# Finishing pieces, transfers, half down tiles and banks: a finer order around an attention loop

## The chip, the cores and the metric

The kernel runs on one core of a Trainium2 chip. The time is device time of one execution, in microseconds (us); for the kernel before it is the median of three runs. One execution was also recorded by the hardware profiler. The engines are named as the profile names them: PE (TensorE, matrix products), PEld (its weight loads), DVE (VectorE), ACT (ScalarE), POOL (GpSimd) and SP (SyncE, which here only issues transfers; "SPq" is its queue). L384 is line 384 of the kernel.

## The reference

The inputs are bf16: x of 2048 rows by 448, caches of 8 key and value heads (2048 keys by 256), and weights. Attention uses 16 query heads, two to each key head, and only the last 512 keys.

```
xn = layernorm(x)
q  = (xn @ wq) as 16 heads of 256
p  = softmax(q @ k.T / 16)                 # k: the last 512 keys
s  = concat_over_heads(p @ v) @ wo
g  = silu((gelu(xn @ w_gate) * (xn @ w_up)) @ w_down)
out = x + s * g
```

## The kernel before

Three stages follow one another. Everything is written into one list of operations by `K.op`, which works out the waits; each engine then runs its own operations in the order of the list. So the order in the code is the order on each engine, and an operation that waits holds up all that stands behind it on its engine, SP's queue included.

**Stage 1, up to about 119 us**: layernorm, the gate and up products and their gelu, with the transposed xn stored to DRAM.

**Stage 2, about 119 to 159 us**, is set by the tuple `order` (L981) and the loop over it (L989). For each head h, `vw_head` computes V_h @ Wo_h (512 x 448), so that the attention later multiplies its probabilities with this and gets the output of wo at once. A head is eight matmuls of 128x448 in four PSUM banks. `vw_mm` (L707) copies them out: of banks j = 0 and j = 1, ACT copies one half and DVE the other less the first (L713, L715); banks j = 2 and 3 are copied by ACT (L719). The banks are filled in the order j = 0, 2, 1, 3. `vw_sums` (L723) then makes three further blocks on DVE. Between the heads stand the last down products of the feed-forward part: tile t of 128 rows is 14 matmuls (`down_mm`, L569), then a tanh on ACT and one DVE operation that make its gate (`down_gate`, L574); `store_g` (L564) sends the gate to DRAM. In `order` a pair is two heads, a float half a down tile, a negative number a whole tile. Heads 14 and 15 come last, with the queries of the first two steps between them.

**Stage 3, about 159 to 551 us**, is the loop of NST = 128 steps (L1037): 8 chunks c of 256 rows (two tiles), 16 heads h each, n = 16 c + h. PE is used as two halves of 64 rows that run side by side; `halves` (L796) deals the matmuls of a step to both. In step n stand on PE the scores of n (`s_jobs`, banks 4 to 6 in turn), the queries of n + 2 (`q_jobs`) and the products of probabilities and V Wo of step m = n - 4 (`pv_jobs`). The 2 x 2 blocks of a product are formed with seven products instead of eight; they need four sums or differences of the probabilities (`sums`, L878, DVE) and are added up over the 16 heads of a chunk in banks 0 to 3: p = 1, 2 in bank 0, p = 6, 7 in bank 1, p = 4, 5 in bank 2, p = 3 in bank 3. In a chunk's first step they start with bank 0, then bank 2 in one half.

The other engines, per step: DVE takes two row minima (L852), the reciprocal of step n - 1's sums (L863) and the sums of step n - 3; ACT takes the copy of the queries and two exponentials (L857); POOL normalises the probabilities of step n - 1 in two instructions (L873); SP issues their transpose (`dma_t`, L375), which step n + 3 uses in its products.

A chunk *ends* at step 16 c + 19, when its last head's products are done. The banks are copied (`evac`, L939, in that step), and `finish` (L947) lists nine pieces, run in the steps after: four POOL additions, a DVE piece `fin(1)` (L962, product with the gate), a POOL piece `add(1)` (L972, plus x), a POOL addition, `fin(0)`, `add(0)`. A step takes a DVE piece from the front of the list, if one is there, behind its sums, and at its end a POOL piece, if one is there. So a DVE piece and the POOL piece behind it fall in one step, and the nine pieces take seven steps. POOL pieces wait for the step's last sum (`after=last_sum`). `add` marks a tile ready; two steps later `store_out` (L934) issues the store of the tile and, through `load_fin` (L930), the two loads (x rows and gate) of the tile four on. At step 4 (`n == LAG`) `load_fin` is called for tiles 0 to 3: eight loads at once. Behind step 115's chunk four steps (118 to 121) also have one more addition each on DVE (`vw_plain`, L1023).

In steps 0 to 3 there are no products yet. There the last two tiles' down products (tiles 14 and 15, half a tile per step) take their place, in bank 0 and 1, and the second half of the queries of steps 2 to 5 goes to bank 3 (the first half to bank 7).

The last chunk's last four products (steps 124 to 127) are done plainly in the tail (L1148), both tiles for each step, in banks 7 and 5; then a product and an addition per tile, DVE and POOL for tile 0, DVE and DVE for tile 1, and the two stores. Of step 127 the two tiles are transposed apart.

Of the kernel before, what the change touches and what calls it, by code (L numbers as in the profile page):

```python
# [166 lines left out]
def bass_recurrent_scan__sliding_block_cached__geglu_ffn__prompt_kernel(  # L167
# [12 lines left out]
    _, S, D = A_x.shape  # L180
# [5 lines left out]
    NT = S // P  # L186
    QC = 512
    NQC = S // QC
    NF = F // P
# [14 lines left out]
    with es:  # L204
# [166 lines left out]
        def dma(q, o, i, reads=(), writes=()):  # L371
            K.op(q, lambda e, o=o, i=i: e.dma_start(o, i), reads, writes, dma=True)  # L372
# [437 lines left out]
        def q_jobs(n, e):  # L810

            c, h = divmod(n, Hq)
            y, i = c % 2, bq(n)
            if e == 1 and 2 <= n < 2 + LAG:
                i = 3
            out = ([], [])
            reads = b_wql[h // HG] + [b_xq[y]]
            for u in range(2):
                rows = slice(R * u, R * u + R)
                for k in [2, 1, 0] + ([NK] if u == e else []):  # L820
                    l = wqr[rows, h, :] if k == NK else wq[rows, k, h * Dh + e * P:h * Dh + (e + 1) * P]
                    out[u].append([i, e * CW, (e + 1) * CW, l, xq[rows, y, k, :], False, False, reads])
            return out

        def q_evac(n):
            s, i = n % NQT, bq(n)
            if 2 <= n < 2 + LAG:
                for e, i in ((0, 7), (1, 3)):
                    act(qT[:, s, e, :], bank[i][:, e * CW:(e + 1) * CW], ACT.Copy, (b_ps[i],), b_qT[s][e:e + 1], scale=NEG)
            else:  # L830
                act(qT[:, s, :, :].rearrange("p e q -> p (e q)"), bank[i], ACT.Copy, (b_ps[i],), b_qT[s], scale=NEG)
# [95 lines left out]
        def load_xq(c):  # L927
            dma("sp", xq[:, c % 2, :, :], xnd[c, :, :, :], b_xnd[2 * c:2 * c + 2], (b_xq[c % 2],))

        def load_fin(t):  # L930
            dma("sp", xr[:, t % NXR, :], x_view[:, t, :], (), (b_xr[t % NXR],))
            dma("sp", gr[:, t % NXR, :], gd[t, :, :], (b_gd[t],), (b_gr[t % NXR],))

        def store_out(t):  # L934
            dma("sp", out_view[:, t, :], ofin[:, t % 2, :], (b_ofin[t % 2],), ())
            if t + NXR < NT:
                load_fin(t + NXR)

# [39 lines left out]
                    ("dve", fin(0)), (eng, add(0))]  # L978


        order = (8.0, (3, 4), 8.5, (5, 6), -9, (7, 8), -10, (9, 10), -11, (11, 12), -12, (2, 13), -13, 14, 15)  # L981
        ring = [0]

        def banks4():
# [2 lines left out]
            return r  # L987

        for k in order:  # L989
            if isinstance(k, tuple):  # L990
                vw_head(k[0], banks4())
                vw_head(k[1], banks4())
                if k[0] in (7, 9):
                    y = k[0] // 8
                    K.reuse(b_xq[y:y + 1])
                    load_xq(y)
            elif isinstance(k, float):
                f = 0 if k == 8 else NF // 2
                down_mm(8, bank[4][:, 0:D], [b_ps[4]], f, f + NF // 2)
                if f:  # L1000
                    down_gate(8, bank[4][:, 0:D], [b_ps[4]])
                    store_g()
            elif k < 0:
                i = 4 + k % 2
                down_tile(-k, bank[i][:, 0:D], [b_ps[i]])
                store_g()
# [30 lines left out]
        for n in range(NST):  # L1037
# [8 lines left out]
            for t in ready:  # L1046
                store_out(t)
            ready, stores = stores, []
            if more:
                q0, q1 = q_jobs(n + 2, 0), q_jobs(n + 2, 1)  # L1050
                q0[1][0][5] = True
                (q1[0] if m >= 0 else q1[1])[-1][6] = True
                if m < 0:
                    q1[0][0][5] = q0[0][-1][6] = True
            if m < 0:
                halves(s0[0] + q1[0] + q0[0] + s1[0], q0[1] + s1[1] + s0[1] + q1[1])
                t, i, f = NT - 2 + n // 2, n // 2, n % 2 * NF // 2
# [44 lines left out]
        assert not todo and not stores and not ready  # L1102

        def add(eng, o, a, b, reads, writes, f=ALU.add):
            K.op(eng, lambda e: e.tensor_tensor(o, a, b, f), reads, writes)
# [39 lines left out]
        add("dve", o, o, gs[1], b_aS[4:6] + b_tmp[1:2], b_aS[4:6], ALU.mult)  # L1145
        add("dve", o, o, xs[1], b_aS[4:6] + [b_xr[ends_at[1]]], b_aS[4:6])
        PB = (7, 5)
        for n in range(NST - LAG, NST):  # L1148
            h, x = n % Hq, n % NPT
            v = vw[:, vslot(h), :, :, :]  # L1150
            for t in range(2):
                i = PB[t]
                mms([(bank[i][:, 0:D].rearrange("p (a n) -> p a n", a=2), pT[:, x, t, j, :],
                      v[:, 0:7:6, j, :] if j < 2 else v[:, 1:3, j % 2, :],
                      n == NST - LAG and j == 0, n == NST - 1 and j == 3) for j in range(4)],
                    [b_late[t] if n == NST - 1 else b_pT[x]] + [b_vw[h][k] for k in (0, 1, 2, 6)], [b_ps[i]])
# [62 lines left out]
```

## Time and profile before

| what | us |
|---|---|
| median of three runs (lowest, highest) | 564.74 (563.42, 565.24) |
| the profiled execution, its own time | 564.22 |
| its span, first to last instruction | 562.4 |
| PE, DVE, ACT, POOL busy | 551.0, 464.3, 341.4, 263.7 |
| one normalisation on POOL (L873, 254 of them) | 0.722 |
| one row minimum on DVE (L852, 256) | 0.683 |
| one exponential on ACT (L857, 256) | 0.684 |
| `fin` on DVE (L962, 14), `add` on POOL (L972, 14) | 0.678, 1.034 |
| SP's issue of a transpose; of a 112 KB transfer | 1.23; 0.43 to 0.57 |
| transposes, issue to landing: lowest, median, highest | 2.5, 3.1, 5.5 |

The page of the profile gives busy times and shares per engine, the waits by who waited for whom, groups of instructions, and the chain of work that ended last. Matmuls overlap in PE's pipeline, so a group's mean is longer than the distance between two of them, and PE counts as busy while one is under way. Stretches between two points of time are given with the busy time and number of instructions of every engine, the granted clock of PE (1.00 is full), the share of the DMA engines and GB/s.

### The profile page before, as it was taken

To read this page: it belongs to the slowest core of one execution; us is meant where nothing else is said; L and a number is where in the kernel's file an instruction comes from. 1 tells how busy PE (TensorE), PEld (TensorE's weight loads), DVE (VectorE), ACT (ScalarE), POOL (GpSimd) and SP (SyncE) were. 2 spreads that over 40 slices of the span, in tenths; PEclk is the share of its full clock that TensorE was granted. 3 is DMA by queue.
4 is the path that set the end of the run, shared out by engine and by line. 5 is a ranking of instruction groups with operands and counts; after the bars stand their busy time and mean duration, and the time that the engine had idled before them with its cause. 6 is when DMAs were issued, how large, how long until landed. Compare 5 with 4: busy or idle time off the path is not lost.

```text
span 562.4 us, 18696 instructions
## 1 busy us (share of the span) xinstructions
PE 551.0 (98%) x7612; PEld 424.6 (75%) x7612; DVE 464.3 (83%) x1177; ACT 341.4 (61%) x811; POOL 263.7 (47%) x376
## 2 busy tenths in 40 slices
PE   8999999999999999999999999999999999999996
PEld 5544444444557898989998898999899889989883
DVE  6674979757767778897998889899888978988996
ACT  5432224567776676666766766666666666666652
POOL 1121580100014444774575466457547736744775
PEclk9999999999999999999999999999999999999999
DMA  9999999201115667477668646545755846664553
GB/s 266 181 242 142 217 323 200 62 1 44 37 28 127 122 82 114 76 132 109 96 108 122 107 81 124 112 98 111 126 98 94 135 90 111 99 124 89 84 111 73
DMA packets 187653, 66.07 MB, mean 117 GB/s; under 512 B 169120, under 2 KB 184624, under 8 KB 187568
## 3 DMA queue, kind: packets, MB, share of 16 engines
q1 hardware_dynamic: 184336, 56.96, 56.6%
q0 software_dynamic: 2464, 7.34, 4.7%
q8 instruction: 60, 0.98, 0.7%
q10 hardware_dynamic: 768, 0.57, 0.3%
q14 instruction: 25, 0.20, 0.1%
HBM read 19.76 MB, written 5.77 MB: 45 GB/s over the span
## 4 chain that ended last, share of the span: by engine, by line
PE 77%; DVE 12%; DMA 6%; issue 2%; ACT 1%; SPq 1%; POOL 1%; DVEq 0%; ACTq 0%
PE bank L384 77%; DMA pT<-pn 5%; DVE sS L888 5%; DVE mn L852 3%; SPq L372 1%; DVE actT L559 1%; DVE tmp L962 1%; DMA x<-in_A_x_dram 1%; DVE mx L676 1%; ACT gl L378 0%; DVE xn L457 0%; DVE stats L431 0%; DVE vw L715 0%; POOL pn L873 0%; ACT L378 0%
## 5 line engine op out<-in xcount | busy, mean ns | idle before, releaser
L384 PE MATMUL bank<-kT,qT 64*128 64x512 bf16 x1024 | 283.3, 376 | 0.0
L873 POOL TENSOR_SCALAR pn<-p,rd 128x512 f16<-128x512 f32 x254 | 180.2, 722 | 179.3 <-DVE rd L863 179.3
L384 PE MATMUL bank<-xq,wq 64*128 64x256 bf16 x1536 | 221.7, 269 | 0.9 <-ACT vw L719 0.8
L384 PE MATMUL bank<-vw,sS 64*128 64x224 f16 x1984 | 218.2, 257 | 0.3 <-DVE sS L888 0.3
L384 PE MATMUL bank<-vw,pT 64*128 64x224 f16 (+1 forms) x1520 | 210.6, 259 | 2.6 <-DMA pT<-pn 2.6
L852 DVE TENSOR_REDUCE mn<-bank 128x1 f32<-128x512 f32 x256 | 172.2, 683 | 38.7 <-PE bank L384 32.4
L857 ACT ACTIVATE p<-bank,mn 128x512 f32<-128x512 f32 x256 | 174.6, 684 | 10.7 <-DVE mn L852 6.3
L384 PEld LDWEIGHTS bank<-vw,sS 64*128 64x128 f16 x1984 | 146.4, 94 | 21.4 <-DVE sS L888 5.1
L384 PEld LDWEIGHTS bank<-vw,pT 64*128 64x128 f16 (+1 forms) x1520 | 142.0, 94 | 8.8 <-PE bank L384 3.4
L384 PEld LDWEIGHTS bank<-xq,wq 64*128 64x128 bf16 x1536 | 140.5, 94 | 10.7 <-ACT vw L719 1.2
L378 ACT ACTIVATE qT<-bank 128x512 bf16<-128x512 f32 (+1 forms) x132 | 77.0, 584 | 117.0 <-PE bank L384 116.0
L384 PEld LDWEIGHTS bank<-kT,qT 64*128 64x128 bf16 x1024 | 87.8, 94 | 6.3 <-ACT p L857 1.2
L384 PE MATMUL bank<-xnT,wgu 64*128 64x512 bf16 (+2 forms) x768 | 84.5, 350 | 1.0 <-issue 0.5
L888 DVE TENSOR_TENSOR sS<-pT 128x256 f16<-128x256 f16 x248 | 74.3, 340 | 3.4 <-DMA pT<-pn 3.4
L384 PE MATMUL bank<-xq,wqr 64*128 64x256 bf16 x256 | 68.3, 269 | 0.0
L384 PEld LDWEIGHTS bank<-xnT,wgu 64*128 64x128 bf16 x768 | 36.7, 94 | 38.5 <-issue 1.3
L378 ACT ACTIVATE gl<-bank 128x512 bf16<-128x512 f32 x56 | 33.1, 597 | 48.8 <-PE bank L384 40.3
L857 ACT ACTIVATION_READ_ACCUMULATOR p<-bank,mn 128x1 f32 x256 | 50.7, 198 | 0.0
L559 DVE TENSOR_TENSOR actT<-bank,gl 128x512 bf16<-128x512 f32 x56 | 37.4, 685 | 15.7 <-PE bank L384 15.1
L384 PE MATMUL bank<-wd,actT 128*128 128x448 bf16 x224 | 44.6, 353 | 0.6 <-DVE actT L559 0.5
L888 DVE TENSOR_TENSOR sS<-sS,pT 128x256 f16<-128x256 f16 x124 | 43.9, 354 | 0.0
L888 DVE TENSOR_TENSOR sS<-pT,sS 128x256 f16<-128x256 f16 x124 | 39.9, 322 | 4.3
(82 smaller groups left out, 405.8 us busy)
## 6 DMA issues: line engine op xcount, KB each, us to landing
wq<-in_A_wq_dram POOLq DMA_DIRECT2D x8, 384.0 KB, 8.9
woa<-in_A_wo_dram POOLq DMA_DIRECT2D x6, 448.0 KB, 6.4
pT<-pn SPq DMA_TRANSPOSE x129, 3.1
xn_t<-xnT SPq DMA_DIRECT2D x16, 128.0 KB, 4.1
xq<-xn_t SPq DMA_DIRECT2D x8, 256.0 KB, 2.9
xr<-in_A_x_dram SPq DMA_DIRECT2D x16, 112.0 KB, 2.5
gr<-gate_t SPq DMA_DIRECT2D x16, 112.0 KB, 2.6
out_dram<-ofin SPq DMA_DIRECT2D x16, 112.0 KB, 2.0
```

The costliest lines, as they stand in the source:

```text
L372: K.op(q, lambda e, o=o, i=i: e.dma_start(o, i), reads, writes, dma=True)
L378: K.op("act", lambda e, o=o, i=i: e.activation(o, i, func, scale=scale), reads, writes)
L384: ins = e.matmul(o, lhsT=l, rhs=r, start=st, stop=sp)
L559: K.op("dve", lambda e: e.tensor_tensor(actT[c % 2][:, f, :], bank[b + 1], gl[:, s, :], ALU.mult), (b_ps[b + 1], b_gl[s]), (b_actT[c % 2][ ...
L676: K.op("dve", lambda e: e.tensor_reduce(mx[:, i:i + 1], o, AX.XY, ALU.max, apply_absolute_value=True), (b,), (b_mx,))
L852: K.op("dve", lambda e: e.tensor_reduce(mn[:, m:m + 1], bank[i], AX.X, ALU.min), (b_ps[i],), (b_mn[m],))
L857: K.op("act", lambda e: e.activation(p32[:, z, :], bank[i], ACT.Exp, bias=mn[:, m:m + 1], scale=-1.0, accum_out=rsum[:, 2 * r + t:2 * r + ...
L873: K.op(engs[t], lambda e, o=o, i=i, s=s: e.tensor_scalar(o, i, s, 1.0, op0=ALU.mult, op1=ALU.mult), (b_p32[z], b_rd[r]), (b_pn[y][t],))
L888: o = K.op("dve", lambda e, i=i, a=a, b=b, f=f: e.tensor_tensor(s[i], a, b, f), r, (b_sS[y][i],))
L962: K.op("dve", lambda e: e.scalar_tensor_tensor(out=tmp[:, s, :].rearrange("p (a n) -> p a n", a=2), in0=aS[:, sl, :], scalar=sc[:, 1:2], i ...
```

## The change

It has five parts.

1. **Finishing pieces**: a step takes one piece from the front of the list, DVE's or POOL's, at its end. The nine pieces take nine steps.
2. **Transfers**: `load_fin` and `store_out` put their transfers into a list `moves`, and each step issues one of them on SP at its start.
3. **Stage 2**: the order is half a down tile, one head, half a down tile, one head, through tiles 8 to 13 and heads 3 to 12, 2, 13; then heads 14 and 15 as before.
4. **Banks in steps 0 to 3**: the second half of the queries goes to bank 1 instead of 3, and tile 15's down product to bank 2 instead of 1.
5. **Last products**: steps 124 and 125 for both tiles as before, then steps 126 and 127 for tile 0, then for tile 1.

```diff
@@ q_jobs @@
             if e == 1 and 2 <= n < 2 + LAG:
-                i = 3
+                i = 1
@@ q_evac @@
-                for e, i in ((0, 7), (1, 3)):
+                for e, i in ((0, 7), (1, 1)):
@@
+        moves = []
+
         def load_fin(t):
-            dma("sp", xr[:, t % NXR, :], x_view[:, t, :], (), (b_xr[t % NXR],))
-            dma("sp", gr[:, t % NXR, :], gd[t, :, :], (b_gd[t],), (b_gr[t % NXR],))
+            moves.append(lambda: dma("sp", xr[:, t % NXR, :], x_view[:, t, :], (), (b_xr[t % NXR],)))
+            moves.append(lambda: dma("sp", gr[:, t % NXR, :], gd[t, :, :], (b_gd[t],), (b_gr[t % NXR],)))
 
         def store_out(t):
-            dma("sp", out_view[:, t, :], ofin[:, t % 2, :], (b_ofin[t % 2],), ())
+            moves.append(lambda: dma("sp", out_view[:, t, :], ofin[:, t % 2, :], (b_ofin[t % 2],), ()))
             if t + NXR < NT:
                 load_fin(t + NXR)
@@
-        order = (8.0, (3, 4), 8.5, (5, 6), -9, (7, 8), -10, (9, 10), -11, (11, 12), -12, (2, 13), -13, 14, 15)
+        heads = [*range(3, 13), 2, 13]
+        order = []
+        for i, h in enumerate(heads):
+            order += [8 + i / 2, h]
+        order += [14, 15]
@@ for k in order @@
+            if isinstance(k, float):
+                t, f = int(k), 0 if k == int(k) else NF // 2
+                i = 4 + t % 2
+                down_mm(t, bank[i][:, 0:D], [b_ps[i]], f, f + NF // 2)
+                if f:
+                    down_gate(t, bank[i][:, 0:D], [b_ps[i]])
+                    store_g()
+            elif k < 14:
+                vw_head(k, banks4())
+                if k in (8, 10):
+                    y = k // 10
                     K.reuse(b_xq[y:y + 1])
                     load_xq(y)
...
@@ for n in range(NST) @@
             for t in ready:
                 store_out(t)
             ready, stores = stores, []
+            if moves:
+                moves.pop(0)()
...
-                t, i, f = NT - 2 + n // 2, n // 2, n % 2 * NF // 2
+                t, i, f = NT - 2 + n // 2, n // 2 * 2, n % 2 * NF // 2
...
-            if todo and todo[0][0] == "dve":
-                todo.pop(0)[1]()
             if n in (1, 3):
                 i = n // 2
-                down_gate(NT - 2 + i, bank[i][:, 0:D], [b_ps[i]])
+                down_gate(NT - 2 + i, bank[2 * i][:, 0:D], [b_ps[2 * i]])
...
-            elif todo and todo[0][0] == "pool":
+            elif todo:
                 todo.pop(0)[1]()
@@ tail @@
-        for n in range(NST - LAG, NST):
+        for n, t in [(n, t) for n in range(NST - LAG, NST - 2) for t in range(2)] + [
+                (NST - 2, 0), (NST - 1, 0), (NST - 2, 1), (NST - 1, 1)]:
...
             store_out(NT - 2 + t)
+            moves.pop(0)()
```

More of the change, by code (lines that the diff above doesn't have):

```diff
@@ L989, in bass_recurrent_scan__sliding_block_cached__geglu_ffn__prompt_kernel @@
         for k in order:
[L990 to L994, printed above, removed]
+            if isinstance(k, float):
[9 more added lines that the diff above has]
+                    y = k // 10
                     K.reuse(b_xq[y:y + 1])
                     load_xq(y)
[L997 to L1006, printed above, removed]
             elif k == 14:
@@ L1101, in bass_recurrent_scan__sliding_block_cached__geglu_ffn__prompt_kernel @@
                 load_xq(c + 1)
-        assert not todo and not stores and not ready
+        assert not todo and not stores and not ready and not moves
         def add(eng, o, a, b, reads, writes, f=ALU.add):
@@ L1147, in bass_recurrent_scan__sliding_block_cached__geglu_ffn__prompt_kernel @@
         PB = (7, 5)
-        for n in range(NST - LAG, NST):
+        for n, t in [(n, t) for n in range(NST - LAG, NST - 2) for t in range(2)] + [
+                (NST - 2, 0), (NST - 1, 0), (NST - 2, 1), (NST - 1, 1)]:
             h, x = n % Hq, n % NPT
             v = vw[:, vslot(h), :, :, :]
[L1151 to L1156, printed above, removed]
+            i = PB[t]
+            mms([(bank[i][:, 0:D].rearrange("p (a n) -> p a n", a=2), pT[:, x, t, j, :],
+                  v[:, 0:7:6, j, :] if j < 2 else v[:, 1:3, j % 2, :],
+                  n == NST - LAG and j == 0, n == NST - 1 and j == 3) for j in range(4)],
+                [b_late[t] if n == NST - 1 else b_pT[x]] + [b_vw[h][k] for k in (0, 1, 2, 6)], [b_ps[i]])
         for t in range(2):
```

## The prediction

> **What bounds the kernel now.** I read the page's busy shares first, then TensorE's waits, then stretches of single steps, then the chain of waits and the timeline around each excess.
>
> ```profile
> PE 551.0 (98%) x7612; PEld 424.6 (75%) x7612; DVE 464.3 (83%) x1177; ACT 341.4 (61%) x811; POOL 263.7 (47%) x376
> ```
>
> TensorE is the bound and is busy to 98%, so the change can only win where it stands still or is issued late. Its waits:
>
> ```profile
> PE bank L384 <- DMA pT<-pn: 2.6, 6, 0.7
> ...
> PE bank L384 <- ACT vw L719: 0.8, 1, 0.8
> PE bank L384 <- DVE vw L715: 0.7, 1, 0.7
> ...
> PE bank L384 <- DVE sS L888: 0.3, 1, 0.3
> ```
>
> That names the places, not the whole price: a matmul that was issued late counts as busy. So I cut the loop at the first score matmul of each step (from the timeline). The columns below are the stretch, its length, busy time by engine, clock, DMA share and GB/s. First line: a quiet step. Second and third: steps 8 and 47. Then steps 25 to 29 of one chunk, step 28 alone, and steps 121 to 125.
>
> ```profile
> 258.39:261.38 2.99, 2.99 (x54) 2.74 (x51) 2.40 (x8) 1.98 (x6) 1.36 (x2) 1.00 0.45 88
> ...
> 185.26:188.92 3.66, 3.22 (x54) 2.69 (x51) 2.43 (x8) 1.99 (x6) 1.36 (x2) 1.00 0.75 160
> 303.81:307.60 3.79, 3.17 (x54) 2.66 (x52) 2.43 (x8) 1.99 (x6) 1.36 (x2) 1.00 0.59 117
> ...
> 285.54:300.82 15.28, 15.28 (x255) 13.62 (x252) 14.71 (x38) 10.19 (x26) 11.34 (x15) 1.00 0.70 115
> 294.64:297.78 3.14, 3.14 (x55) 2.65 (x53) 3.11 (x8) 2.30 (x6) 2.83 (x5) 1.00 0.87 94
> 529.76:545.68 15.92, 15.85 (x254) 13.36 (x252) 15.35 (x40) 10.19 (x26) 11.54 (x16) 1.00 0.47 97
> ```
>
> A step is 2.99 us when only TensorE limits it. Above that lie 0.67 (step 8), 0.80, 0.40, 0.56 and 0.38 (steps 47, 62, 95, 111, all waits for pT), 15.28 - 14.96 = 0.32 in each of the six chunks' finishes (all six stretches are 15.28), and 15.92 - 14.96 = 0.96 in the last. In the finishes VectorE is busy 14.71 of 15.28: there it is the bound. The chain shows why step 8 is late:
>
> ```profile
> 174.93 1.37 POOL pn L873 x2
> 176.36 1.23 SPq L375
> 177.65 0.57 SPq L372
> ...
> 181.76 0.43 SPq L372
> 182.24 3.98 DMA pT<-pn
> ```
>
> Eight loads stand on SP's queue between two transposes, 177.65 to 182.19, 4.54 us, and the transpose behind them lands at 186.22, while a quiet one lands 3.04 us after its issue. The timeline around the hand-over, and two pairs on the port:
>
> ```profile
> 160.26 0.63 ACT L719 ACTIVATE vw<-bank,sc 128x448 f16<-128x448 f32 x1
> 160.95 0.28 PE L384 MATMUL bank<-xq,wq 64*128 64x256 bf16 x1 [0.79 <-ACT vw L719]
> ...
> 173.99 0.35 PE L384 MATMUL bank<-vw,pT 64*128 64x224 f16 x2
> 174.14 0.62 DVE L581 SCALAR_TENSOR_TENSOR g2r<-tmpr,bank 128x448 bf16<-128x448 f32 x1 [0.51 <-PE bank L384]
> ...
> 228.66 0.70 DVE L888 TENSOR_TENSOR sS<-sS,pT 128x256 f16<-128x256 f16 x1
> 227.61 1.60 POOL L873 TENSOR_SCALAR pn<-p,rd 128x512 f16<-128x512 f32 x2
> ...
> 558.95 0.90 DVE L1105 TENSOR_TENSOR ofin<-p,aS 128x448 bf16<-128x448 f32 x1
> 558.24 1.13 POOL L1105 TENSOR_TENSOR ofin<-p,aS 128x448 bf16<-128x448 f32 x1 [1.89 <-DVE p L1105]
> ```
>
> **The change part by part**, against the profiled execution's own 564.22 us (span 562.4); the median of the three runs, 564.74, is 0.5 above it.
>
> *One transfer per step, first burst.* The eight loads now leave one each in steps 5 to 12. Each costs SP 0.43 to 0.57 us, and SP's quiet step holds one transpose of 1.23 in 2.99, so it goes in SP's idle time. Behind it in the queue stands only the next transpose, whose slack in a quiet step is 3.2 us (lands 3.2 before the step that uses it). Step 8 loses its 0.67. Bounds: 0 to 0.67 gained; I take 0.66.
>
> *One transfer per step, stores and reloads.* Each finished tile now sends store, xr load and gr load in three steps, no longer in one (0.57 + 0.43 + 0.45 plus gaps = 1.6 us of SP). The transpose of step 44 shows what this adds up to: issued at 299.69 behind three transfers and a late POOL, landed at 304.90 (5.21 us), 4.4 us later than a quiet one. POOL's lateness is the other half: in the old step with both a VectorE and a POOL piece, POOL starts its add only when the VectorE piece ends, and the two normalisations (1.65) and their transpose leave 2.2 us later than in quiet steps (5.0 against 2.8 after the step's start). With one piece the lateness is that of the steps with a POOL piece alone, 0.8 to 1.4 us, and in the 35 such steps of the seven finishes no TensorE wait occurred, though single landings took up to 4.5 us. The waits of steps 47, 62, 95, 111, 0.80 + 0.40 + 0.56 + 0.38 = 2.14, should go. Long landings (5.47 us at 200.73 with no other transfer near) will stay, at other places. Bounds: 0 (all waits return elsewhere) to 2.14; I take 2.1, since the nearest rows show none.
>
> *One piece per step.* No piece is added; nine steps hold what seven held. A step with a POOL piece alone has VectorE busy 2.56 to 2.61 and lasts 2.99. One with the 0.68 us VectorE piece (0.60 in the pipe) has 2.97 and lasts 3.00. The excess stands in the steps after, where POOL's add of 1.03 and normalisations of 1.65 run beside the sums and VectorE needs 3.03 to 3.11. After the change a step of 2.97 is followed by one of about 2.6, so the 0.6 us backlog is worked off before the sums hold up the products. Per chunk 0.32 can go; I take 0.25 (the copies of step 19 and 20 stay), six times: 1.5. In the last chunk four extra additions of 0.30 to 0.39 us lie in steps 118 to 121 beside the pieces, so some backlog stays: of 0.96 I take 0.6. Bounds together: a loss of 0.7 (nothing goes, and each of the fourteen adds, which get a step of their own, makes that step 3.04, as the one at 297.78 is) to 1.92 + 0.96 = 2.9 gained. Taken: 2.1.
>
> Here the Trainium skill speaks against the change. "SBUF — State Buffer", section "Who interferes with whom", says that a VectorE instruction with two SBUF inputs fully blocks against a GpSimd instruction that reads SBUF. The trace's row is 0.70 instead of 0.28 us, so a block of 0.42. By the page a sum could lose a whole POOL instruction, and the sum would be some tenths of a us worse per chunk; by the row it is not.
>
> *Half tiles between single heads.* Work on TensorE is the same: per head and half tile, (3.06 + 2.65)/2 = 2.86 us. The copies out of a head run as a chain on VectorE (0.44, 0.61 waiting for ScalarE, 0.45, sums to 1.03: 2.58 per head, 0.54 more per tile), so 5.70 per two heads against TensorE's 5.71. Today the pair behind the first half tile outruns it and waits 0.70 at 128.10. With 1.33 us of down product ahead of every head this wait goes, and head 15 ends at about 158.65 instead of 159.36. At the end heads 13 and 14 stand back to back without cover. The first queries need head 13's last two banks. The chain starts a head 121.88 - 120.61 = 1.3 us after its matmuls and frees these banks 1.5 later, 2.8 in all; TensorE gets there after two heads, 3.07. So I cost it at nothing, covered by head 14; lateness above 1.5 us would be paid in full.
>
> *First queries in bank 1.* At 160.95 TensorE waited for the fourth copy of head 15 (ends 160.89) because the second half of query 2 writes bank 3. Bank 1 holds the second copy, which ended at 159.87: 1.0 us earlier. Step 0 lasts 4.24 against 3.16 for steps 1 to 3. What comes late next is bank 4: step 1's second score needs the exponential of step 0's first (162.74 to 163.42), and that follows the sums of head 15 (end 162.02), which come only about 0.5 earlier. Step 1 now reaches that score at 164.0, with 0.6 to spare. So both gains together are at least 0.5 and at most 0.5 + 0.6 = 1.1; I take 1.0.
>
> *Tile 15 in bank 2.* This adds a wait. Step 4's products go to bank 0 and then, as fifth, to bank 2: today that matmul starts at 173.99, 0.82 us into the step. The gate of tile 15 reads its bank until 174.76 (tanh, then the 0.62 us piece). Today it reads bank 1, which the products reach at 175.19, 2.0 us into the step. In bank 2 TensorE waits 174.76 - 173.99 = 0.77, with everything of step 4 queued behind. Nothing gives it back. Bounds: 0 to 0.9 lost; I take 0.8.
>
> *Last products by tiles.* The matmuls are the same and so is their end (8 of 128x448 in 1.69, the last at about 558.2); tile 0's four end 0.77 earlier, at 557.4. Its transpose landed at 555.38, so moving it ahead waits for nothing. Its product and POOL's add then run before tile 1's VectorE add, which today takes 0.90 beside POOL's 1.13; the same work without POOL takes about 0.62. Gain 0.3 (0 to 0.6).
>
> Sum: 0.66 + 2.1 + 2.1 + 1.0 - 0.8 + 0.3 = 5.36, so 564.2 - 5.4 = 558.8 in a profiled execution, 559.3 as a median.
>
> **Rivals.** (a) *Waits return*: landings stretched by other traffic, not the bursts, make the waits, and they come back where POOL is 1.4 late. For it: 5.47 us with nothing near. Against it: no wait in the 35 steps above. Price 2.1, so 561.4 as a median. (b) *The uncovered heads cost*: heads 13 and 14 each bring 2.58 of copying against 1.54 of matmuls, 1.04 short each. If the chain has no slack there, 2.1 us come back in place of the 1.0 gain: 562.4. Against it: TensorE's 0.7 lead. (c) *It does nothing in the finish*: VectorE stays the bound in it, since its total is unchanged; 2.1 stay: 561.4. Against it: 14.71 of 14.96 would still fit. (d) *Slower*: a lone transfer stretches the transpose beside it. The place is 46 steps, not 15. Landings beside three transfers took 3.0 to 5.2 us. If each of the 46 landed 2.2 late as the worst did, that would pass the smallest slack, 1.8, by 0.4; 0.4 x 46 = 18 us of waits, so 577. It decides once the mean wait passes 5.4/46 = 0.12 us. Against it: the six transposes just ahead of the one 256 KB load of queries landed in 3.05 to 4.38, median 3.3.
>
> **How the numbers follow.** Forecast 0.64 (its own range 557.6 to 560.6), (a) 0.13, (b) 0.11, (c) 0.07, (d) 0.05. 0.3% is 1.7 us, about what a measurement of this kernel can tell from no change: faster is below 563.0. Forecast, (a), (c) and half of (b), less 0.03 for two rivals at once, are faster: 0.87; the other half of (b) and the 0.03 are the same: 0.08; (d) is slower: 0.05. The range goes from the gains near their upper bounds together (7.4 us, 557.4) to (b) (562.3), which leaves out (d), rivals together and a little below.
>
> **What would show it.** After: no step of 3.66 at step 8 and loads one per step on SP; steps 25 to 29 of a chunk within 15.1; no pT waits but the one of 0.7 in the last products; step 0 about 3.5; a new TensorE wait of about 0.8 in step 4, put down to the gate of tile 15; VectorE's last add near 0.6. I am wrong if TensorE waits before the first queries, or if pT waits still sum to over 2 us.

## The result and the profile after

After the change the median is 559.86 us (559.46 to 560.55, four runs), against 564.56 us for the kernel before in the same session. The ratio is 0.992, 95% interval 0.990 to 0.994: faster by 4.7 us. The profiled execution took 560.09 us, its span is 558.3 us, 4.1 below the 562.4 of before. The prediction was a median of 559.3 us, 0.6 below the measured one, from gains that sum to 5.36 in the span; there the gain, 4.1, is 1.2 us short of the forecast, and the terms must be looked at one by one.

First the page's busy line of after, then TensorE's waits (engine and line, what it waited for, us in total, times, longest):

```profile
PE 548.5 (98%) x7612; PEld 425.5 (76%) x7612; DVE 462.3 (83%) x1177; ACT 341.3 (61%) x811; POOL 261.5 (47%) x376
```

```profile
PE bank L384 <- DMA pT<-pn: 1.5, 1, 1.5
...
PE bank L384 <- DVE g2r L581: 0.5, 1, 0.5
PE bank L384 <- ACT p L857: 0.5, 1, 0.5
```

The six idle waits for pT (the transposed probabilities) have become one, in the last products, and that one has doubled (0.7 before). Two new waits stand at the start of the loop: for the gate of tile 15, and for an exponential that nobody waited for before. The stretches, with the columns as before: stage 2 from its first half down tile to step 0, then steps 0, 1, 4 and 8, steps 25 to 29, steps 121 to 125:

```profile
119.34:158.67 39.33, 39.16 (x224) 20.13 (x225) 29.15 (x73) 30.95 (x64) 0.00 (x0) 1.00 0.11 32
...
158.67:162.27 3.60, 3.45 (x30) 1.78 (x30) 2.67 (x7) 2.50 (x6) 0.00 (x0) 1.00 0.00 0
162.27:166.15 3.88, 3.42 (x30) 1.92 (x30) 2.16 (x5) 3.15 (x9) 1.37 (x2) 1.00 0.00 0
172.48:176.38 3.90, 3.40 (x52) 2.72 (x53) 2.27 (x6) 1.76 (x5) 1.36 (x2) 1.00 0.44 97
185.41:188.45 3.04, 3.04 (x54) 2.74 (x51) 2.40 (x8) 2.01 (x6) 1.36 (x2) 1.00 1.14 93
284.97:299.94 14.97, 14.97 (x254) 13.70 (x252) 14.11 (x38) 10.05 (x26) 9.86 (x14) 1.00 0.55 105
525.51:540.86 15.35, 15.32 (x254) 13.44 (x250) 14.86 (x40) 10.09 (x26) 10.14 (x14) 1.00 0.58 95
```

Step 8 is down from 3.66 to 3.04, the finish from 15.28 to 14.97, the last from 15.92 to 15.35. Step 4 is up from 3.06 to 3.90, step 1 from 3.16 to 3.88. For the table, stage 2, steps 0 and 1, steps 2 to 4, and step 126 with the tail, all of before; then the last of these in after:

```profile
119.28:159.44 40.16, 39.39 (x224) 19.80 (x224) 29.34 (x74) 30.58 (x65) 0.00 (x0) 1.00 0.10 31
159.44:166.84 7.40, 6.61 (x59) 3.74 (x59) 4.63 (x10) 5.26 (x14) 1.37 (x2) 1.00 0.00 0
166.84:176.23 9.39, 9.39 (x110) 6.71 (x110) 5.97 (x15) 6.50 (x18) 4.02 (x6) 1.00 0.52 110
545.69:562.41 16.72, 11.60 (x108) 6.86 (x102) 12.18 (x28) 4.90 (x14) 9.27 (x13) 0.98 0.39 81
...
540.86:558.30 17.44, 11.78 (x108) 6.80 (x104) 12.29 (x28) 4.92 (x14) 10.50 (x15) 1.00 0.51 84
```

Stage 1 alone moved the start of stage 2 by up to 1.2 us between the kernels of this study (118.85 to 120.06), so I compare lengths of stretches, not points of time.

| stretch | before | after | gain found | gain predicted |
|---|---|---|---|---|
| stage 1 | 119.28 | 119.34 | -0.06 | 0 |
| stage 2 and steps 0, 1 | 40.16 + 7.40 | 39.33 + 7.48 | 0.75 | 1.0 |
| steps 2 to 4 | 9.39 | 10.23 | -0.84 | -0.8 |
| step 8 | 3.66 | 3.04 | 0.62 | 0.66 |
| waits for pT in later steps | 2.14 | 0.21 | 1.93 | 2.1 |
| six finishes, steps 25 to 29 | 6 x 15.28 | 6 x 14.97 | 1.87 | 1.5 |
| last finish, steps 121 to 125 | 15.92 | 15.35 | 0.57 | 0.6 |
| step 126 and the tail | 16.72 | 17.44 | -0.72 | +0.3 |
| sum | | | 4.12 | 5.36 |

Every term of the loop holds within 0.4. The tail has the wrong sign, and that is where most of the missing 1.2 us lies.

### The profile page after: what moved, and what is told of

The parts are those of the page before. It is cut to its first block, busy times and chain, and to the rows that moved or that the text cites. A ratio compares the mean times of both kernels' runs of the same rounds, so it can differ in the third digit from the quotient of the medians.

```text
span 558.3 us, 18692 instructions
## 1 busy us (share of the span) xinstructions
PE 548.5 (98%) x7612; PEld 425.5 (76%) x7612; DVE 462.3 (83%) x1177; ACT 341.3 (61%) x811; POOL 261.5 (47%) x376
## 4 chain that ended last, share of the span: by engine, by line
PE 88%; DVE 7%; ACT 2%; issue 2%; DMA 1%; POOL 0%; DVEq 0%; ACTq 0%
PE bank L384 88%; DVE vw L726 1%; DVE vw L715 1%; DVE actT L559 1%; DMA pT<-pn 1%; ACT vw L713 1%; DVE mx L676 1%; DMA x<-in_A_x_dram 1%; DVE stats L431 1%; DVE xn L457 1%; ACT gl L378 0%; DVE sS L888 0%; DVE mn L852 0%; DVE g2a L581 0%; POOL rstd L443 0%
## 5 line engine op out<-in xcount | busy, mean ns | idle before, releaser
L873 POOL TENSOR_SCALAR pn<-p,rd 128x512 f16<-128x512 f32 x254 | 178.3, 714 | 177.8 <-DVE rd L863 177.8
L888 DVE TENSOR_TENSOR sS<-sS,pT 128x256 f16<-128x256 f16 x124 | 46.8, 377 | 0.0
L955 POOL TENSOR_TENSOR aS<-aS 128x224 f32<-128x224 f32 (+1 forms) x35 | 29.8, 850 | 27.7 <-DVE rd L863 25.8
```

The lines of the kernel that those rows point to most:

```text
L873: K.op(engs[t], lambda e, o=o, i=i, s=s: e.tensor_scalar(o, i, s, 1.0, op0=ALU.mult, op1=ALU.mult), (b_p32[z], b_rd[r]), (b_pn[y][t],))
L888: o = K.op("dve", lambda e, i=i, a=a, b=b, f=f: e.tensor_tensor(s[i], a, b, f), r, (b_sS[y][i],))
L955: K.op(eng, lambda e: e.tensor_tensor(sl[0], sl[1], sl[2], ALU.add), [b_aS[i] for i in a + b], [b_aS[i] for i in o], after=last_sum)
```

## The experiments

Ratios are to the kernel before in the same session, with 95% intervals. The medians are from several sessions, so two changed kernels are compared by their ratios, or by spans and stretches of their profiled executions.

**One transfer per step, alone.** The kernel before with `moves` and nothing else:

```diff
+        moves = []
...
-            dma("sp", out_view[:, t, :], ofin[:, t % 2, :], (b_ofin[t % 2],), ())
+            moves.append(lambda: dma("sp", out_view[:, t, :], ofin[:, t % 2, :], (b_ofin[t % 2],), ()))
...
+            if moves:
+                moves.pop(0)()
```

> The kernel before with part 2 alone (one transfer per step). Common to both theories: step 8 goes from 3.66 to about 3.0 us (-0.6), the six finishes stay at 15.28 us, steps 0 to 4 stay. Theory A (the bursts of three transfers made the waits for pT in steps 47, 62, 95 and 111): these 2.14 us go although POOL is as late as before (transposes issued 5.0 us after the step's start), so the span is 562.4 - 0.6 - 2.1 = 559.7 and the ratio 0.995. Theory B (POOL's lateness, from a step with two pieces, made them): at least 1.5 us of waits for pT stay in steps 24 to 31 of the chunks, the span is 561.2 or more and the ratio at least 0.998.

Measured: 561.73 us, ratio 0.9962 (0.995 to 0.9975), span 560.1. Step 8's excess goes. Five of the six finishes stay at 15.28 (the sixth, with a longer step 108, takes 15.53). Of the four waits for pT three go and one stays, step 62. The first stretch is that step, the second steps 25 to 29 of one chunk's finish:

```profile
348.26:351.75 3.49, 3.16 (x54) 2.65 (x52) 2.43 (x8) 1.99 (x6) 1.36 (x2) 1.00 0.85 180
284.55:299.83 15.28, 15.28 (x254) 13.62 (x252) 14.71 (x38) 10.19 (x26) 11.35 (x15) 1.00 0.66 107
```

SP's queue tells the two apart. Before, ahead of the transpose for step 43, on which step 47 waited (start, us, queue, operation):

```profile
298.03 0.58 SPq L372 DMA_DIRECT2D out_dram<-ofin  x1
...
299.13 0.46 SPq L372 DMA_DIRECT2D gr<-gate_t  x1
299.69 5.15 SPq L375 DMA_TRANSPOSE pT<-pn  x3
```

and in this run:

```profile
297.04 0.57 SPq L372 DMA_DIRECT2D gr<-gate_t  x1
297.70 1.23 SPq L375 DMA_TRANSPOSE pT<-pn  x1
```

The transpose for step 43 left 5.05 us after step 44's start before and leaves 4.04 after it here; it landed in 5.21 us and now in 3.16. It is still later than in a quiet step (2.8), because the transpose ahead of it on SP is as late as before. The wait of step 95 is of the same kind. The transpose for step 58, on which step 62 waits, had no burst ahead of it: it left 5.14 after its step's start and still leaves at 5.13, since POOL is as late as ever, and lands in 4.88.

The wait of step 111 is a case of its own. Its transpose landed in a usual 3.21 us, but left 6.63 after its step's start, because one load in the burst ahead of it kept SP for 2.04 us:

```profile
494.55 2.04 SPq L372 DMA_DIRECT2D gr<-gate_t  x1
```

In the two runs below that leave transfers and pieces as they were (half tiles alone, banks alone), this load took its usual time, the transpose left at 4.91, and step 111 does not wait, while steps 47, 62 and 95 do. So neither theory holds for all four: two waits were the burst's on top of a late POOL, one was POOL's, and the 0.38 of step 111 belongs to the one profile of before and tests neither.

**One piece per step, alone:**

```diff
-            if todo and todo[0][0] == "dve":
-                todo.pop(0)[1]()
...
-            elif todo and todo[0][0] == "pool":
+            elif todo:
                 todo.pop(0)[1]()
```

> The kernel before with part 1 alone (one finishing piece per step). Common: step 8 stays at 3.66 us, the six finishes go from 15.28 to 14.96 (-1.9), the last from 15.92 to about 15.35 (-0.6), the wait for the transpose in the last products grows from 0.7 to about 1.5 because the last finishing addition now stands two steps later on POOL, ahead of the scaling of the gates (+0.8). Theory A (bursts): over 1 us of waits for pT stays, span 562.4 - 2.5 + 0.8 = 560.7, less up to 1: ratio 0.995 to 0.997. Theory B (POOL's lateness): the 2.14 us of waits go as well, span 558.6, ratio 0.993.

Measured: 560.31 us, ratio 0.994 (0.9921 to 0.9959), span 558.4: theory B to 0.2 us. All four waits go although the bursts remain. The bursts stand ahead of other transposes now, since the two `add` pieces come one and two steps later; the 12 transposes of the loop with three transfers right ahead leave 4.1 to 5.0 after their step's start, and the latest lands 9.07 after it. In the waits of steps 47, 62 and 95 of before it was 9.90 to 10.26. Step 8, one finish, the last finish:

```profile
185.06:188.87 3.81, 3.22 (x54) 2.68 (x52) 2.43 (x8) 1.99 (x6) 1.36 (x2) 1.00 0.77 168
285.19:300.16 14.97, 14.97 (x256) 13.70 (x252) 14.11 (x38) 10.05 (x26) 9.86 (x14) 1.00 0.62 112
525.72:541.08 15.36, 15.33 (x255) 13.45 (x251) 14.88 (x40) 10.10 (x26) 10.14 (x14) 1.00 0.57 96
```

With the nine-step finish the transpose for step 43 leaves 3.73 after step 44's start. In those three waits lateness and a long landing (4.8 to 5.2 us) came together; to take away POOL's part of the lateness is enough. Step 126 and the tail are 17.37 here, 0.65 longer than before, without any change to the last products: the first sign of where the tail's loss comes from.

**Half tiles alone, banks alone.** The kernel before with the order of half down tiles and single heads; then the kernel before with the two bank changes:

```diff
-        order = (8.0, (3, 4), 8.5, (5, 6), -9, (7, 8), -10, (9, 10), -11, (11, 12), -12, (2, 13), -13, 14, 15)
+        heads = [*range(3, 13), 2, 13]
+        order = []
+        for i, h in enumerate(heads):
+            order += [8 + i / 2, h]
+        order += [14, 15]
...
```

> The kernel before with part 3 alone (half down tiles between single heads). Theory A (the prediction): the wait of 0.70 us in the first heads goes, heads 13 and 14 without cover cost nothing, step 0 starts about 0.7 us earlier, at 158.65; what of it the end sees depends on the wait for the fourth copy of head 15, which stays in step 0: span 561.7 to 562.1. Rival (uncovered heads cost): step 0 starts no earlier or later than 159.36 and the span is 562.4 or more, up to 564.5.

```diff
-                i = 3
+                i = 1
...
-                t, i, f = NT - 2 + n // 2, n // 2, n % 2 * NF // 2
+                t, i, f = NT - 2 + n // 2, n // 2 * 2, n % 2 * NF // 2
...
```

> The kernel before with part 4 alone (second half of the queries of steps 2 to 5 in bank 1, tile 15 in bank 2). Theory A (the prediction, each part by itself): the wait of 0.79 us in step 0 goes, of which 0.5 us reach step 2; step 4 grows by 0.84 us from the wait for tile 15's gate; the span is 562.4 - 0.5 + 0.84 = 562.7. Theory B (what the trace after suggests: the next in line is the exponential of step 0, which comes no earlier): step 0 is shorter by 0.6 but step 1 longer by as much, step 2 starts as before, the span is 563.2.

Measured: 563.28 us, ratio 0.9996 (0.9986 to 1.0006), and 563.46 us, ratio 0.9997 (0.9987 to 1.0006); neither can be told from no change by its time. The stretches can: stage 2, steps 0 and 1, steps 2 to 4 (before: 40.16, 7.40, 9.39). Half tiles alone, where steps 2 to 4 stay at 9.38:

```profile
119.13:158.47 39.34, 39.17 (x225) 20.10 (x226) 29.15 (x73) 30.96 (x64) 0.00 (x0) 1.00 0.10 32
158.47:166.31 7.84, 6.61 (x60) 3.74 (x60) 4.82 (x11) 5.64 (x15) 1.37 (x2) 1.00 0.00 0
```

Banks alone, with step 8 as the last line:

```profile
118.94:159.12 40.18, 39.40 (x224) 19.78 (x225) 29.36 (x74) 30.58 (x65) 0.00 (x0) 1.00 0.10 31
159.12:166.16 7.04, 6.64 (x59) 3.79 (x59) 4.64 (x10) 5.32 (x14) 1.37 (x2) 1.00 0.00 0
166.16:176.38 10.22, 9.73 (x109) 6.63 (x110) 6.07 (x15) 6.49 (x18) 4.07 (x6) 1.00 0.48 101
...
185.41:188.46 3.05, 3.05 (x55) 2.72 (x53) 2.45 (x8) 2.02 (x6) 1.36 (x2) 1.00 0.66 132
```

The half tiles gain 0.82 in stage 2, so heads 13 and 14 cost nothing that shows without cover; 0.44 of it is given back in step 0, which leaves 0.38. The query bank gains 0.36. Together after has 0.75: they add up. Of the expectations for the banks, theory A was nearer: its 0.5 was 0.36, and theory B's zero is wrong. Tile 15's bank costs 0.83 here and 0.84 in after, all in step 4. But here step 8 gives 0.62 of it back: the eight loads still go at once, yet with step 4 so much longer the transpose behind them leaves 5.04 after step 5's start, not 6.01, and lands just in time. Neither expectation saw this; it is one reason why the span is 561.7 and not 562.7 or more. In after nothing is given back, because step 8 has no excess left.

**The last products in the old order,** the rest as after:

```diff
-        for n, t in [(n, t) for n in range(NST - LAG, NST - 2) for t in range(2)] + [
-                (NST - 2, 0), (NST - 1, 0), (NST - 2, 1), (NST - 1, 1)]:
+        for n in range(NST - LAG, NST):
...
+            for t in range(2):
```

> The kernel after with part 5 undone (the last products in the old order, step by step). The tail, from the first score of step 127 to the end, is 14.49 us after and 13.88 before. Theory A (the order by tiles gains the predicted 0.3, and the loss in the tail comes from the finishing pieces through a late transpose): the tail grows to about 14.8, VectorE's last addition is 0.9 us again. Rival (the order by tiles itself lost it): the tail returns to about 13.9 and the ratio to after is 0.999.

Measured: 559.47 us, ratio 0.9926 (0.9911 to 0.9941), the same as after. The tail is 14.38, which is neither 14.8 nor 13.9. The reason is the transpose for step 125: it took 4.89 us to land in after and 4.48 here. The run with the sums of heads 14 and 15 later (below) has the order by tiles and the same landing of 4.48, the same issue (3.96 and 3.95 after the step's start) and the same wait; step 126 and the tail are 17.06 there against 17.34 here. TensorE's last products and VectorE's last two operations with the old order:

```profile
548.94 4.71 PE L384 MATMUL bank<-vw,pT 128*128 128x448 f16 x24 [1.07 <-DMA pT<-pn]
...
552.93 1.38 DVE L1107 TENSOR_TENSOR p<-bank,tmp 128x448 f32<-128x448 f32 x2 [1.06 <-PE bank L384]
554.35 0.90 DVE L1107 TENSOR_TENSOR ofin<-p,aS 128x448 bf16<-128x448 f32 x1
```

and with the order by tiles at the same landing:

```profile
548.56 4.71 PE L384 MATMUL bank<-vw,pT 128*128 128x448 f16 x24 [1.07 <-DMA pT<-pn]
...
551.79 0.62 DVE L1109 TENSOR_TENSOR p<-bank,tmp 128x448 f32<-128x448 f32 x1 [0.31 <-PE bank L384]
553.31 0.62 DVE L1109 TENSOR_TENSOR p<-bank,tmp 128x448 f32<-128x448 f32 x1 [0.89 <-PE bank L384]
553.97 0.62 DVE L1109 TENSOR_TENSOR ofin<-p,aS 128x448 bf16<-128x448 f32 x1
```

From the wait's end to VectorE's end it is 6.31 us with the old order and 6.03 with the new. So the order by tiles gains its predicted 0.3 (the last addition takes 0.62, as predicted, in place of 0.90), by one profile of each, and the rival is out.

**The gates' scaling off POOL,** the rest as after:

```diff
-                K.op("pool", lambda e, s=s, y=y: e.tensor_scalar(
-                    tmp[:, s, :], gr[:, y, :], sc[:, 1:2], 1.0, op0=ALU.mult, op1=ALU.mult),
-                    (b_gr[y], b_sc), (b_tmp[s],))
+                act(tmp[:, s, :], gr[:, y, :], ACT.Copy, (b_gr[y], b_sc), (b_tmp[s],), scale=sc[:, 1:2])
```

> The kernel after, with the scaling of the last two tiles' gates (L1034, 1.30 us on POOL, just behind the last finishing addition) on ScalarE instead. Theory A (this scaling and the addition together make the transpose for step 125 late): that transpose leaves 0.6 to 1.3 us earlier after its step's start, the wait for it falls from 1.48 us to 0.2 to 0.9, the tail from 14.49 to 13.2 to 13.9 us. Rival (the long landing of 4.9 us makes the wait, and it stays): tail above 14.3 us.

Measured: 558.39 us, ratio 0.9903 (0.9887 to 0.992). The profiled execution was the longest of the four, 559.75 us; its stage 1 alone took 0.72 more than in after. POOL in after, from the last finishing addition (L974) to the normalisations for step 125:

```profile
539.48 1.03 POOL L974 TENSOR_TENSOR ofin<-tmp,xr 128x448 bf16<-128x448 f32 x1 [0.95 <-DVE rd L863]
540.49 1.51 POOL L873 TENSOR_SCALAR pn<-p,rd 128x512 f16<-128x512 f32 x2
541.98 1.30 POOL L1034 TENSOR_SCALAR tmp<-gr,sc 128x448 f32<-128x448 bf16 x2
543.26 1.46 POOL L873 TENSOR_SCALAR pn<-p,rd 128x512 f16<-128x512 f32 x2
```

and in this run:

```profile
539.95 1.04 POOL L974 TENSOR_TENSOR ofin<-tmp,xr 128x448 bf16<-128x448 f32 x1 [0.95 <-DVE rd L863]
540.96 1.51 POOL L873 TENSOR_SCALAR pn<-p,rd 128x512 f16<-128x512 f32 x2
543.11 1.36 POOL L873 TENSOR_SCALAR pn<-p,rd 128x512 f16<-128x512 f32 x2 [0.63 <-DVE rd L863]
```

In after POOL runs four things on end without a gap; here it idles 0.63 before the normalisations. The transpose for step 125 leaves 3.22 after its step's start, not 3.93, the wait falls from 1.48 to 1.04, step 126 and the tail from 17.44 to 16.64. It took 4.81 to land. So theory A holds in the lateness, although the long landing stays; the wait (1.04) and the tail (13.94) end just above the ranges that it gave.

**The sums of heads 14 and 15 later,** the rest as after:

```diff
-                vw_head(k, (0, 1, 2, 3))
+                vw_head(k, (0, 1, 2, 3), False)
...
+            if n in (1, 2):
+                vw_sums(13 + n)
```

> The kernel after, with the sums of heads 14 and 15 of V Wo (two times 1.03 us on VectorE ahead of step 0's row minimum) moved behind the row minima of steps 1 and 2. Theory A (VectorE's chain in front of the first row minimum sets step 2's start, not the queries' bank and not the half tiles): the first row minimum starts about 1 us earlier than 161.69, steps 0 and 1 together fall from 7.48 to 6.4 to 6.8 us, 0.7 to 1.1 less, and the span to about 557.4. Rival (ScalarE's order sets it, the copies of the queries ahead of head 15's copies): steps 0 and 1 together stay above 7.2 us.

Measured: 559.33 us, ratio 0.9921 (0.9906 to 0.9936): no gain over after, whose ratio is 0.992. Steps 0 and 1 together, then steps 2 to 4, then step 3 alone:

```profile
158.20:164.97 6.77, 6.61 (x61) 3.74 (x60) 3.55 (x7) 5.53 (x15) 1.37 (x2) 1.00 0.00 0
164.97:175.91 10.94, 9.98 (x110) 6.59 (x111) 8.18 (x21) 6.53 (x18) 4.09 (x6) 1.00 0.44 94
168.13:172.03 3.90, 3.42 (x31) 1.93 (x31) 3.76 (x11) 3.16 (x9) 2.35 (x4) 1.00 0.44 96
```

Theory A holds: 7.48 becomes 6.77, so VectorE's chain in front of the first row minimum set step 2's start. But 0.7 comes back in step 3. By its total, VectorE had room there: it is busy 1.93 of 3.17 us in step 3 of after. Here it is busy 3.76 of 3.90, because the sums of each head run in one piece, 1.11 and 1.32 us, ahead of the row minima of steps 2 and 3 in the list, and hold them up.

**Five edits at once.** Tile 15 in bank 3, the gates as above, the sums as above, the four extra additions of the last chunk in steps 113, 114, 117 and 118, and the copies of a finished chunk dealt out anew:

```diff
                 evac(0, "dve")
+                evac(1, "act")
                 evac(2, "act")
...
-                evac(1, "dve")
-                evac(3, "act")
+                evac(3, "dve")
```

> The kernel after with five edits in places apart: tile 15 in bank 3 (step 4 from 3.90 to 3.06 us, -0.84), gates scaled on ScalarE (-0.6 to -1.3 in the tail), sums of heads 14 and 15 later (-0.7 to -1.1), the four extra additions on VectorE in steps 113, 114, 117 and 118 in place of 118 to 121 (step 122 from 3.38 to 3.0, -0.38), and of a finished chunk bank 1 copied by ScalarE and bank 3 by VectorE (steps 16 c + 19 and 16 c + 20 from 3.05 and 3.15 to about 3.0: -0.2 in each of seven chunks; or a loss, if the exponentials behind ScalarE's extra copy hold up the scores). Sum -3.6 to -4.9 if each goes: span 553.4 to 554.7. Rival: the copies cost as much as they give, span about 556.

Measured: 561.98 us, ratio 0.9969 (0.9957 to 0.998), span 560.0: slower than after, by 1.7 in the span. Step 4 is 3.06 as expected. The copies cost it: step 20 and its like, 3.15 before and after, take 3.76 in each of seven chunks, 4.3 us in all:

```profile
220.36:224.12 3.76, 3.56 (x54) 2.65 (x52) 2.78 (x9) 3.20 (x8) 0.95 (x2) 1.00 0.48 111
```

VectorE is indeed less busy (2.78, not 3.02), but ScalarE's second copy stands ahead of its two exponentials, VectorE's reciprocal waits for the second of them, and the next row minima stand behind the reciprocal. ScalarE's copies, and VectorE's idle time of 0.94:

```profile
220.56 0.98 ACT L378 ACTIVATE aS<-bank 128x448 f32<-128x448 f32 x2 [0.49 <-PE bank L384]
```

```profile
222.91 0.17 DVE L863 RECIPROCAL rd<-rsum 128x2 f32<-128x2 f32 x1 [0.94 <-ACT p L857]
```

The first row minimum comes 2.63 after the step's start, not 2.01. This is the loss that the expectation left open, on another way than it named: through the reciprocal, not straight from exponential to score.

**Four edits, and a fifth.** The same without the copies, and the six sums spread, one in each of steps 5 to 10; then the last finishing addition held back to step 126 as well:

```diff
+            if 5 <= n < 11:
+                vw_sums(14 + (n - 5) // 3, (((5, 2, 4), (6, 5, 0), (3, 1, 5))[(n - 5) % 3],))
...
-                t, i, f = NT - 2 + n // 2, n // 2 * 2, n % 2 * NF // 2
+                t, i, f = NT - 2 + n // 2, n // 2 * 3, n % 2 * NF // 2
...
-        VW12 = {NST - Hq + 6 + i: Hq - LAG + i for i in range(LAG)}
+        VW12 = {NST - Hq + k: Hq - LAG + i for i, k in enumerate((1, 2, 5, 6))}
...
```

> The kernel after with the edits that held, without the swap of the copies: tile 15 in bank 3; gates scaled on ScalarE; the four extra additions in steps 113, 114, 117 and 118; and the six sums of heads 14 and 15 spread, one in each of steps 5 to 10 (VectorE there is busy 2.41 of 2.99 us and a sum takes 0.39, so 2.80). Theory A (each place has its own price): step 4 at 3.06 (-0.84), steps 0 and 1 together at 6.76 (-0.72) with steps 2 and 3 at 3.16 and steps 5 to 10 at 2.99 to 3.04, step 122 at 3.0 to 3.1 (-0.3), step 126 and the tail at 16.7 (-0.76): span 558.3 - 2.6 = 555.7, within 0.5 for the start of the loop, ratio to before 0.988. Rival (the time comes back in VectorE's next full step, as the sums did in step 3): above 557.

```diff
+            if n == NST - 1:
+                for t in ready:
+                    store_out(t)
+                ready = []
...
-            elif todo:
+            elif todo and n not in (NST - 4, NST - 3):
                 todo.pop(0)[1]()
+            if n == NST - 2:
+                gate_scaled(0)
```

> The same, but the last finishing addition waits on POOL until step 126's normalisations are under way (POOL idles 1.14 us there), its store goes ahead of the transpose for step 126, and ScalarE scales the two gates in steps 123 and 126. Theory A: the transpose for step 125 leaves 0.4 us earlier than in the run beside it, since VectorE's sums of step 124 no longer run beside the addition and the normalisations; the wait in the tail falls from 1.0 to about 0.6 us: span 0.4 below that run. Rival (the landing of 4.8 us or the store in front of the next transpose gives it back): no difference within 0.2 us, or slower.

Measured: 557.09 us, ratio 0.9883 (0.9868 to 0.9898), span 555.3, and 556.96 us, ratio 0.9879 (0.9862 to 0.9895), span 555.3. The first is the forecast of theory A to 0.4 us. Steps 0 and 1, steps 2 to 4, and step 6 with one of the sums:

```profile
158.87:165.63 6.76, 6.61 (x59) 3.74 (x59) 3.55 (x7) 5.51 (x15) 1.37 (x2) 1.00 0.00 0
165.63:175.02 9.39, 9.39 (x109) 6.71 (x110) 5.97 (x15) 6.50 (x18) 4.01 (x6) 1.00 0.52 110
178.01:181.06 3.05, 3.05 (x55) 2.75 (x53) 2.61 (x9) 2.02 (x6) 1.36 (x2) 1.00 0.76 132
```

Both losses of the hand-over are gone and nothing came back. The second kernel does what was meant up to step 127 (the transpose for step 125 leaves 2.78 after its step's start, not 3.19, and step 126 lasts 2.25, not 2.68) and then gives it back: the store of tile 12 now stands ahead of the transpose for step 126, which leaves 3.81 after its step's start, not 3.02, and the tail is 14.16, not 13.62:

```profile
546.18 1.69 PE L384 MATMUL bank<-vw,pT 128*128 128x448 f16 x8 [0.76 <-DMA pT<-pn]
548.21 2.06 PE L384 MATMUL bank<-vw,pT 128*128 128x448 f16 x10 [0.34 <-DMA pT<-pn]
```

One wait has become two, as the rival said. The kernel with four edits is 6.7 us faster than the one before in its session, and its span is 3.0 shorter than that of the kernel with the change (555.3, not 558.3).

## Why the prediction was right or wrong

- **First burst**: right, 0.62 of 0.66; one transfer per step alone brings it too.
- **Stores and reloads**: right in size, 1.93 of 2.1, but the prediction took bursts and POOL's lateness for two halves of each wait, and they were not. Steps 47 and 95 needed both, and either part alone takes these waits away. Step 62 had no burst: one piece per step removes it, one transfer per step does not. Step 111 came from one load that kept SP for 2.04 us, where the prediction counted 0.43 to 0.57; its 0.38 is also gone where neither part was made (there step 108 takes 0.30 more instead), so to count it as a gain of this part was right by luck. The gain of steps 47 and 95 belongs to both parts and must be counted once: alone they gain 1.8 and 3.3 us by the medians, a sum which has it twice. One wait of 0.21 came at a new place (step 32, a landing of 5.28), as foreseen.
- **One piece per step**: the mechanism was right and the size too small. I took 0.25 per chunk; the backlog is worked off entirely and 0.31 goes. The pessimistic bound (each addition's step at 3.04) did not occur: all five steps last 2.99. The last finish gave 0.57 of 0.6.
- **Half tiles and first queries**: 0.75 of 1.0. The step that failed is that the sums of head 15 "come only about 0.5 earlier" and that step 1 has "0.6 to spare". The first row minimum came 0.33 earlier (161.69 after 162.02) while step 0 came 0.77 earlier, so the spare was used up and step 1 waits 0.46 for the exponential behind that minimum. What is late next was named correctly; the term was mis-sized, and the run with the sums moved away shows that it was this chain. Rival (b) is out: stage 2 got shorter by 0.83.
- **Tile 15 in bank 2**: right, 0.84 lost, at the place named and for the reason named. By the runs with bank 3 it need not have been (step 4 at 3.06). "Nothing gives it back" holds in after, but in the run with the banks alone step 8 gives back 0.62.
- **Last products by tiles**: right by itself (0.3), but step 126 and the tail got 0.72 longer. The step that failed is in another part: in costing the nine-step finish I looked at what each piece does inside its chunk and not at what the last chunk's last addition is moved onto. Two steps later it lies right before the scaling of the gates on POOL, and the transpose for step 125, which has no later step to hide in, leaves 0.58 later. The run with pieces alone shows it (+0.65), the run with the scaling on ScalarE takes it back. Another 0.4 is a longer landing of this one transpose (4.89 for 4.47), which the other kernels with this lateness do not show (4.48 to 4.51).

Rivals (a), (c) and (d) did not happen either: of the 50 transposes of after with one 112 KB transfer right ahead, 41 landed in 3.04 to 3.9 us, the latest in 5.28, and no pT wait but the two named was left. The misses of 1.02 (tail), 0.25 (hand-over) and 0.17 (waits) and four of at most 0.06, against 0.37 more than expected from the six finishes, make up the difference of 1.24 between the two sums.

The prediction weighed a rule (the Trainium skill, "SBUF — State Buffer", section "Who interferes with whom", two-input VectorE instructions against GpSimd's reads) and held that its row of 0.70 us, a block of 0.42, speaks against a block for a whole POOL instruction. It does not: that sum begins at 228.66 and ends at 229.36, 0.15 after the two normalisations end (227.61 to 229.21), so what it lost is what was left of the second. Spread over more steps, the two meet less. Of the 496 sums for the products 66 take over 0.5 us in before and with one transfer per step alone, 53 in after and with one piece per step alone. The busy times of the same 1177 VectorE and 376 POOL instructions are 464.3 and 263.7 us in before, 462.6 and 261.5 with one piece per step alone, 462.3 and 261.5 in after.

## What to carry to other kernels

When work is spread over more steps, follow its last piece to the end of the program: in the middle there is a next step to hide in, at the end there is none. A step that gives up a wait needs the room of the engine that is late next written down beside it (VectorE had 0.58 us free in steps 5 to 10, enough for one sum of 0.39 each), and the room must lie behind what others wait for: in step 3 over 1 us was free, but sums in one piece held up the row minima. Two causes that need each other must not be counted twice. A wait that is read off one profile may belong to that profile alone, as that of step 111 did. Where several small edits touch different places, compare stretches: those that an edit left alone agreed to 0.02 us between the kernels (steps 2 to 4 at 9.38 or 9.39, a nine-step finish at 14.96 or 14.97), while whole times of one kernel scatter by 1 us.

## What was not expected of the hardware

The transpose for step 125 lands late in every kernel of the study, 4.47 to 4.89 us after its issue, while the one before it takes 3.04 to 3.11 and the one behind it 3.2 to 3.6. Between the kernels its issue moved by 1.2 us against the steps (2.78 to 3.96 after the start) and by over 3 us against the nearest store without changing this. Other landings of 4 to 5.5 us come at much the same steps in every kernel (79 and 112, for example), also where no other transfer of the kernel is near.

The traces show what goes with them. The profile counts 60 packets of 16 KB, 0.98 MB in all, on a queue of kind "instruction", in the loop of after 6.4 to 11.6 us apart, and 25 smaller ones on a second such queue. Over the twelve profiled executions the loop and the tail have 1548 transposes, and 273 of them land later than 4 us; each of the 273 has a packet of this kind under way between its issue and its landing. The 593 without one land in 3.84 us or less, in the median 3.05. For step 125 such a packet begins 1.93 to 2.37 us after the issue in every kernel, and the transpose lands 2.45 to 2.6 after the packet's start, so the 0.4 by which the landing in after was longer goes with a packet that began 0.4 later (2.37, and 1.97 in before). No run moved the packets, so that they make the long landings is likely but not shown.

Step 108 took 3.43 us, and 3.13 in before, in three of the runs with the seven-step finish. Its third sum on VectorE took 0.69 us there beside a normalisation of POOL, and 0.28 in before, where the pair of normalisations took 1.66 us in place of 1.51 instead; why the two met in another order there stays open.
